# Block-product mixing in an adaLN block: sums and low parts moved to VectorE in pieces of 1536 columns

## The chip, the cores and the metric

The kernel runs on one core of a Trainium2 chip. The metric is the device time of one execution in microseconds (us), shown as the median of several runs. The engines are named as in the profile: PE (TensorE, matmuls), PEld (its weight loads), DVE (VectorE), ACT (ScalarE), POOL (GpSimd) and SP (SyncE, which here issues almost all DMAs). Each engine works through its own queue in order.

## What is computed

One transformer block on 2048 tokens of width 448, in float32: layernorm with modulation, attention with 16 heads of width 28, and a gated MLP whose gate mixes tokens with a 2048 x 2048 matrix.

```python
h = _layernorm(x) * (1 + ca) + sa
x = x + ga * _A_ref(h, A_wqkv, A_wo)             # attention, 16 heads
h = _layernorm(x) * (1 + cb) + sb
z = _gelu(h @ w_in)                              # 2048 x 1792
z1, z2 = z[:, :896], _layernorm(z[:, 896:])
g = w_sp @ z2 + b_sp[:, None]                    # the mixing, 2048 x 2048 by 2048 x 896
x = x + gb * ((z1 * g) @ w_out)
```

## The kernel before

The order on every engine is written out by hand, and the pools of buffers set the waits. A product of two float32 operands is made of three one-pass matmuls in `F32R`: each operand is split into a high part (`hi`, a rounded copy made by ACT) and a low part (`lo`, the operand minus `hi`, made by DVE or POOL in `sub`), and PE sums hi by hi, hi by lo and lo by hi.

The stages follow each other on PE: projections and the first row maxima; attention (256 slots of 4 score tiles, 4 tiles for the row maxima of a later head, and 4 products with V; a slot is one head and one block of 128 keys); the output projection; z1 (28 units of 11 matmuls, `z1_unit`, from weights `w_in`); z2 (16 tiles, `z2_gemm` and `z2_norm`); the mixing; and y, the product with `w_out` (16 tiles of 21 matmuls, `y_part`).

The mixing does not multiply 4 x 4 blocks of `w_sp` (512 x 512 each) with the blocks of z2 directly. For two of three column groups of z2 (384 columns each) it uses 26 products of sums of blocks, listed in `MIX`: each entry holds the sums of z2 blocks to form (`T0`, `T1` are kept, `ONCE` is used by one product only), the block that is multiplied and its sign, the weight (an index into `W_SUMS` for a sum of blocks of `w_sp`, or a pair for a plain block), and the output blocks (column group c, token block tb, sign) to which the product is added. A product p is four steps g = 4p + kt (kt the block of 128 rows), and a step is 9 matmuls of 512 columns into three PSUM banks. The third group of 128 columns (`F6_AT`) adds 3 matmuls to 64 of the 104 steps. So the stage has 104 x 9 + 64 x 3 = 1128 matmuls. Products with even and odd p use two sets of three banks. Per step the loop calls, in this order: `w_load(g + 4)` (SP), `w_split(g + 2)` (hi and lo of the weights), `z_split(g + 4)` (hi and lo of one 384-column piece of z), `evac(p - 1, kt)` (adds one bank of the product before to its outputs `cE`, `cC`, `cF`, `cD`), `z_sum(g + 6)`, gates, and the matmuls in `mix_step(g)`.

POOL makes the z sums (`z_sum`) and the low parts of the weights (`w_split`); DVE makes the low parts of z (`z_split`) and of the third group's weights, and all additions to the outputs. For weights that are sums, the low parts of kt 0 and 1 come ready from DRAM (`wl_scr`), so only kt 2 and 3 have a low part to make. Weight tiles go through few buffers:

```python
PARTS = {"h": (2048, 5), "l": (4608, 4), "p": (6144, 3)}   # hi, lo, ready lo: offset, buffers
raws[g] = [wp.tile([128, 512], F32, name="raw_sp", bufs=5)]
```

The sums of `w_sp` blocks are made during attention: `ws_load` (two loads), `ws_add` (POOL, for 44 of the 112 pieces also hi and lo), `ws_store`, with three pairs of buffers. Attention also needs POOL for the row maxima of each head: `m_max` (DVE, then three short POOL instructions, `mxv` and `mxp`) and in the same slot `m_fin` (a PE transpose `mtp`, a DVE copy `nt`, two small DMAs `qst<-nt` on SP that the head's scores wait for). The slot is the 13th of a head (12 modulo 16).

The output weights are split during the mixing and y starts (`wout_load`, `wout_gate`, `wout_part`); the gate by z1 (`gate`) and the split of the result (`u_split`, which makes `uT`) run tile by tile at the end of the mixing and between the y tiles.

Of the kernel before, what the change touches and what calls it, by code (L numbers as in the profile page):

```python
# [62 lines left out]

T0, T1, ONCE = 8, 9, 10
# [28 lines left out]
ROWS = (0, 2, 3, 1)  # L93
# [4 lines left out]
def tile_adaln_mha_gmlp(ctx, tc, x, wqkv, wo, w_in, w_spT, b_sp, w_out, cT, w_mod0, w_mod, out):  # L98
# [13 lines left out]
    ws_scr = scr.tile([4 * len(W_SUMS), 128, 512], F32, name="ws_scr")  # L112
    wl_scr = scr.tile([2 * len(W_SUMS), 128, 512], F32, name="wl_scr")
# [734 lines left out]
    ws_raw = spool.tile([128, 6, 512], F32, name="ws_raw")  # L848

    def ws_tiles(i):  # L850
        return [ws_raw[:, 2 * (i % 3) + j, :] for j in range(2)]

    def ws_load(i):
        v, kt = divmod(i, 4)
        for t, src in zip(ws_tiles(i), W_SUMS[v][:2]):
            sp.dma_start(t, ws_scr[4 * src + kt] if isinstance(src, int) else w_block(*src, kt))

    def ws_add(i):
        v, kt = divmod(i, 4)
        a, b = ws_tiles(i)  # L860
        pool.tensor_tensor(out=a, in0=a, in1=b, op=ALU.add if W_SUMS[v][2] > 0 else ALU.subtract)  # L861
        if v in W_OPERANDS and kt < 2:
            hi = b.bitcast(F32R)
            pool.tensor_copy(hi, a)
            sub(pool, hi, a, hi)

    def ws_store(i):
        v, kt = divmod(i, 4)
        a, b = ws_tiles(i)
        sp.dma_start(ws_scr[i], a)  # L870
        if v in W_OPERANDS and kt < 2:
            sp.dma_start(wl_scr[2 * v + kt], b)
# [290 lines left out]
    win_load(1, t3b)  # L1163
    for g in range(NG):
        for f in range(7):
            z1_unit(g, f)
            if g == 0 and f == 4:
# [53 lines left out]

    zt = [dpool.tile([128, 8 * 896], F32, name=f"z2{i}", tag=f"heapD{i}") for i in range(2)]
    z2 = [zt[i // 8][:, i % 8 * FH : (i % 8 + 1) * FH] for i in range(NT)]

    once = {}

    def z_reg(r, g):
        kt = g % 4
        if r == ONCE:
            return once[g]  # L1230
        if r >= T0:
            return tsum(r - T0)[:, kt * 384 : (kt + 1) * 384]
        return z2[4 * ROWS[r % 4] + kt][:, FG[r // 4]]

    def z_sum(g):
        if g >= KS:
            return
        for d, a, b, op in MIX[g // 4][0]:
            if d == ONCE:
                once[g] = wp.tile([128, 384], F32, name="once")  # L1240
# [4 lines left out]
    def z_split(g):  # L1245
        if g >= KS:
            return
        _, r, sign, _, _ = MIX[g // 4]
        src, (hi, lo) = z_reg(r, g), zs(g)
        if sign > 0:  # L1250
            act.activation(hi, src, AF.Copy)
            sub(dve, lo, src, hi)
        else:
            act.activation(hi, src, AF.Copy, scale=-1.0)
            dve.scalar_tensor_tensor(out=lo, in0=src, scalar=-1.0, in1=hi.bitcast(F32), op0=ALU.mult, op1=ALU.subtract)
        once.pop(g, None)

    def z6_split(t):
        act.activation(z6h[:, t, :], z2[t][:, FG[2]], AF.Copy)
        sub(dve, z6l(t), z2[t][:, FG[2]], z6h[:, t, :])  # L1260
# [34 lines left out]
    def w_split(g):  # L1295
        for key, eng in ((g, pool), (("f", g), dve)):
            if key in raws:
                raw = raws.pop(key)
                hi = w_part("h")
                act.activation(hi, raw[0], AF.Copy)  # L1300
# [32 lines left out]

    for t in range(NT + 1):
        if t < NT:
            z2_gemm(t)
        if 0 < t <= NT:
            z2_norm(t - 1)
        if t == 8:
            heapB2.append(fh.tile([128, 8 * 896], F32R, name="heapB2", tag="heapB"))  # L1340
            tbuf.append(wp.tile([128, 5120], F32, name="tbuf", tag="tw", bufs=1))
        if 9 <= t < 13:
            z_sum(t - 9)
            b_load(bts(t - 9), t - 9)
        if 10 <= t < 14:
            z_split(t - 10)
        if t >= 9:
            z6_split(2 * t - 18)
            z6_split(2 * t - 17)
# [5 lines left out]
    for g in range(4, 6):  # L1355
        z_sum(g)
# [12 lines left out]
    acc, acc6 = {}, {}  # L1369
    F6_ENDS = {tb: (min(gs), max(gs)) for tb in range(4) for gs in [[g for g in F6_AT if F6_AT[g][0] == tb]]}  # L1370

    def mix_step(g):
        p, kt = divmod(g, 4)
        if p < 2 and kt == 0:
            acc[p] = [bank("acc") for _ in range(3)]
        zh, zl = zs(g)
        hi, lo = wsp.pop(g)
        for f in range(3):
            c, o = slice(f * 128, (f + 1) * 128), acc[p % 2][f]
            pe.matmul(o, zh[:, c], hi, start=p < 2 and kt == 0, stop=False, skip_group_check=p > 1)  # L1380
            pe.matmul(o, zh[:, c], lo, start=False, stop=False, skip_group_check=p > 1)  # L1381
            pe.matmul(o, zl[:, c], hi, start=False, stop=kt == 3, skip_group_check=p > 1)  # L1382
        if g in F6_AT:
# [3 lines left out]
            side = tb in (2, 3)  # L1387
            if side not in acc6:
                acc6[side] = ps_o.tile([128, 512], F32, name="acc6", tag="o") if side else bank("acc6")
            o, t = acc6[side], 4 * ROWS[k] + kt  # L1390
# [8 lines left out]
    def evac(p, f):  # L1399
        for c, tb, sign in MIX[p][4]:  # L1400
            u = utile(3 * c + f, tb)
            d_add(u, u if (c, tb) in started else bts(tb), acc[p % 2][f], ALU.add if sign > 0 else ALU.subtract)
            if f == 2:
                started.add((c, tb))
# [21 lines left out]
    def u_split(f, tb):  # L1426
        if tb not in uTs:
            uTs[tb] = hview(dpool.tile([128, 8 * 896], F32R, name="uT", tag=f"heapD{(1, 0, 1, 0)[len(uTs)]}"), 0, 14, 512)
        uT, u = uTs[tb], utile(f, tb)
        act.activation(uT[:, f, :], u, AF.Copy)  # L1430
        sub(dve, uT[:, 7 + f, :], u, uT[:, f, :])

    x2t, yps = {}, {}

    wraws = {}

    def wout_load(f):
        wraws[f % 2] = wp.tile([128, D], F32, name="wraw_o", bufs=2)
        sp.dma_start(wraws[f % 2], w_out[f * 128 : (f + 1) * 128, :])

    def wout_gate(f):
        d_add(wraws[f % 2], wraws[f % 2], bcs["gb"], ALU.mult)

    def wout_part(f):
        if f == 0:
            tbuf.append(wp.tile([128, 5120], F32R, name="wouts", tag="tw", bufs=1))
        act.activation(wouts_h(f), wraws[f % 2], AF.Copy)
        sub(dve, wouts_l(f), wraws[f % 2], wouts_h(f))
# [5 lines left out]
    def y_part(t, end=False):  # L1454
        ts, uT = slice(t % 4 * 128, t % 4 * 128 + 128), uTs[t // 4]
        y = bank("y_ps")
# [9 lines left out]
    GATE_AT = (69, 70, 71, 76, 77, 79, 81, 83, 92, 93, 94, 95, 96, 97, 98, 99, 100)  # L1466
    WOUT_LOAD = (48, 49, 60, 61, 97, 99, 101)
    WOUT_GATE = (50, 51, 62, 63, 98, 100, 102)
    WOUT_PART = (51, 52, 63, 64, 100, 101, 103)

    for g in range(KS):
# [3 lines left out]
        z_split(g + 4)  # L1475
        if p and kt < 3:
            evac(p - 1, kt)
        z_sum(g + 6)
# [6 lines left out]
        if g >= 97:  # L1485
            u_split((6, 3, 4, 5, 0, 1, 2)[g - 97], 2)
        for fn, at_g in ((wout_load, WOUT_LOAD), (wout_gate, WOUT_GATE), (wout_part, WOUT_PART)):
            if g in at_g:
                fn(at_g.index(g))
# [5 lines left out]
    ts = [8, 9, 10, 11, 4, 5, 6, 7, 12, 13, 14, 15, 0, 1, 2, 3]  # L1495
    splits = [(f, 1) for f in (6, 0, 1, 2, 3, 4, 5)] + [(f, 3) for f in (3, 4, 5, 0, 1, 2, 6)] + [(f, 0) for f in (0, 1, 2, 6, 3, 4, 5)]
    for f in range(3):
        evac(NM - 1, f)
    for k, t in enumerate(ts):
        if k + 2 < len(ts):  # L1500
            x2_load(ts[k + 2])
        if k < 12:
            for _ in range((1, 1, 1, 1, 2, 2, 2, 1, 0, 0, 0, 0)[k]):
                gate()
                z1_load()
            for _ in range((2, 2, 2, 1)[k % 4]):
                u_split(*splits.pop(0))
        y_part(t, k == 15)

# [51 lines left out]
```

## Time and profile before

| | |
|---|---|
| time, three runs | 1414.46, 1417.89 and 1422.31 us; median 1417.89 |
| profiled execution | 1415.37 us, span 1413.6 us, mean granted clock 0.995 |
| busy | PE 1382.3, PEld 976.0, DVE 1086.3, ACT 816.7, POOL 535.8 us |
| moved by DMA | 247.89 MB |
| mixing on PE | from 1058.1 us of the span to 1341 us |

The profile has one row per group of instructions (line, engine, operation, output and input tiles, count, busy time, mean duration, idle time before and what ended it), a list of waits (who waited for whom: total, times, longest), and windows (busy time of each engine in a stretch, then the granted PE clock, the DMA share and GB/s). A PE that is 98% busy is the bound over most of the span; its matmuls overlap, so their mean duration (0.39 us for 512 columns) is longer than the distance from one to the next.

### The profile page before, as it was taken

How to read it: one execution, taken by the hardware profiler on the slowest of the kernel's cores; microseconds unless marked ns; L12 is line 12 of the kernel's file. 1: busy time of each engine (PE TensorE's matmuls, PEld its weight loads, DVE VectorE, ACT ScalarE, POOL GpSimd, SP SyncE). 2: the span in 40 equal slices, each digit the busy share in tenths (PEclk: the TensorE clock that was granted, in tenths of full speed). 3: DMA queues.
4: the chain of work that ended last, by engine and by line, in shares of the span. 5: the costliest groups of instructions: out<-in, count | busy, mean ns of one | idle time of the engine just before them, and what ended most of it. 6: DMA issues, size and time to landing. Idle time of an engine off the chain costs nothing. (4 is left out here: it accounts for less than half of the span.)

```text
span 1413.6 us, 20902 instructions
## 1 busy us (share of the span) xinstructions
PE 1382.3 (98%) x7098; PEld 976.0 (69%) x7098; DVE 1086.3 (77%) x1788; ACT 816.7 (58%) x1578; POOL 535.8 (38%) x499
## 2 busy tenths in 40 slices
PE   9999999999999999999999999999999999888998
PEld 8888655555555555555555545888997888666798
DVE  7898888888888888888888841840469779987962
ACT  6623666777766666776776678452245545544421
POOL 2134334233436254344533351000149456844400
PEclk9999999999999999999999999999999999999999
DMA  7464756666666666666577542533206756676553
GB/s 276 142 182 171 211 143 179 184 174 199 187 193 174 199 195 188 189 175 192 185 201 215 187 155 73 177 130 124 89 16 218 220 181 208 200 229 192 182 182 98
DMA packets 133048, 247.89 MB, mean 175 GB/s; under 512 B 21385, under 2 KB 33291, under 8 KB 130395
## 3 DMA queue, kind: packets, MB, share of 16 engines
q1 hardware_dynamic: 130222, 242.37, 56.5%
q10 hardware_dynamic: 2718, 4.19, 0.8%
q8 instruction: 56, 0.92, 0.3%
q14 instruction: 52, 0.42, 0.1%
HBM read 171.32 MB, written 70.38 MB: 171 GB/s over the span
## 5 line engine op out<-in xcount | busy, mean ns | idle before, releaser
L710 DVE TENSOR_REDUCE pm<-mt 128x1 f32<-128x512 f32 x1024 | 631.3, 682 | 86.0 <-PE mt L705 86.0
L741 ACT ACTIVATE P<-st_ps 128x512 f32<-128x512 f32 x1024 | 515.7, 626 | 210.1 <-PE st_ps L737 209.4
L737 PE MATMUL st_ps<-qst,kst 128*128 128x512 f32 x1024 | 406.4, 406 | 3.3 <-DMA qst<-nt 2.8
L705 PE MATMUL mt<-kst,qst 128*128 128x512 f32 x1024 | 402.5, 393 | 0.0
L737 PEld LDWEIGHTS st_ps<-qst,kst 128*128 128x128 f32 x1024 | 191.2, 188 | 146.0 <-issue 96.2
L861 POOL TENSOR_TENSOR ws_raw<-ws_raw 128x512 f32<-128x512 f32 x112 | 144.2, 1288 | 323.6 <-DMA ws_raw<-in_w_spT_dram 177.4
L752 PE MATMUL o_ps<-P,V 128*32 128x512 f32 x2048 | 247.5, 601 | 0.0
L705 PEld LDWEIGHTS mt<-kst,qst 128*128 128x128 f32 x1024 | 192.4, 188 | 31.6
L1300 ACT ACTIVATE heapB<-raw_sp 128x512 fp32r<-128x512 f32 x156 | 97.5, 629 | 129.3 <-issue 41.9
L752 PEld LDWEIGHTS o_ps<-P,V 128*32 128x32 f32 x2048 | 53.7, 109 | 124.0 <-issue 118.6
L1380 PE MATMUL acc<-heapB,heapA 128*128 128x512 f32 x312 | 123.1, 395 | 11.3 <-ACT heapB L1300 5.6
L147 POOL TENSOR_TENSOR heapB<-raw_sp,heapB 128x512 fp32r<-128x512 f32 x60 | 85.2, 1424 | 109.4 <-ACT heapB L1300 91.1
L1382 PE MATMUL acc<-heapB,heapA 128*128 128x512 f32 x312 | 122.4, 392 | 0.0
L1381 PE MATMUL acc<-heapB,heapA 128*128 128x512 f32 x222 | 87.4, 394 | 8.4 <-DVE heapB L147 5.2
L1380 PEld LDWEIGHTS acc<-heapB,heapA 128*128 128x128 f32 x312 | 59.1, 190 | 27.4 <-ACT heapB L1300 7.7
L147 DVE TENSOR_TENSOR heapB<-raw_sp,heapB 128x512 fp32r<-128x512 f32 x52 | 53.8, 1034 | 22.4 <-ACT heapB L1300 21.2
L1382 PEld LDWEIGHTS acc<-heapB,heapA 128*128 128x128 f32 x312 | 59.0, 189 | 12.1
L400 PE MATMUL pq<-heapD,heapD 128*128 128x512 f32 x196 | 61.9, 390 | 0.0
L147 POOL TENSOR_TENSOR ws_raw<-ws_raw 128x512 fp32r<-128x512 f32 x44 | 56.5, 1285 | 3.5
L1320 DVE BATCH_NORM_STATS2 stz<-z 128x6 f32<-128x448 f32 x32 | 20.0, 626 | 47.8 <-ACT z L1319 47.5
L167 POOL TENSOR_TENSOR rsz<-rsz,mhalf 128x1 f32<-128x1 f32 x16 | 14.6, 914 | 109.0 <-DMA tbuf<-in_b_sp_dram 64.7
L1381 PEld LDWEIGHTS acc<-heapB,heapA 128*128 128x128 f32 x222 | 41.8, 188 | 18.9 <-DVE heapB L147 6.1
(224 smaller groups left out, 1832.0 us busy)
## 6 DMA issues: line engine op xcount, KB each, us to landing
ws_raw<-in_w_spT_dram SPq DMA_DIRECT2D x136, 256.0 KB
ws_scr<-ws_raw SPq DMA_DIRECT2D x112, 256.0 KB
ws_raw<-ws_scr SPq DMA_DIRECT2D x88, 256.0 KB
raw_sp<-ws_scr SPq DMA_DIRECT2D x88, 256.0 KB
raw_sp<-in_w_spT_dram SPq DMA_DIRECT2D x68, 256.0 KB
wl_scr<-ws_raw SPq DMA_DIRECT2D x44, 256.0 KB
kst<-qk_scr SPq DMA_DIRECT2D x45, 224.0 KB
qst<-qk_scr SPq DMA_DIRECT2D x45, 224.0 KB
```

Source lines behind the costliest of these rows:

```text
L147: eng.tensor_tensor(out=dst, in0=a, in1=hi.bitcast(F32), op=ALU.subtract)
L400: pe.matmul(pq, wqk[:, b, m * 128 : (m + 1) * 128], hT[g][:, a, :], start=j == 0, stop=j == NST - 1)
L705: pe.matmul(mt, qst[h % 3][:, t * 128 : (t + 1) * 128], kst[h % 3][:, kb * 512 : (kb + 1) * 512], start=True, stop=True)
L710: dve.tensor_reduce(out=pms[h][:, t, kb : kb + 1], in_=mt, axis=AX.X, op=ALU.max)
L737: pe.matmul(st, kst[h % 3][:, kt * 128 : (kt + 1) * 128], qst[h % 3][:, qb * 512 : (qb + 1) * 512], start=True, stop=True)
L741: act.activation(p, st, AF.Exp, scale=SCALE)
L752: pe.matmul(otile[h][32 * qb : 32 * qb + 32, :], V[:, kt, h, :], ptiles.pop((u, qb)), start=kt == 0, stop=kt == NT - 1)
L861: pool.tensor_tensor(out=a, in0=a, in1=b, op=ALU.add if W_SUMS[v][2] > 0 else ALU.subtract)
L1300: act.activation(hi, raw[0], AF.Copy)
L1380: pe.matmul(o, zh[:, c], hi, start=p < 2 and kt == 0, stop=False, skip_group_check=p > 1)
L1381: pe.matmul(o, zh[:, c], lo, start=False, stop=False, skip_group_check=p > 1)
L1382: pe.matmul(o, zl[:, c], hi, start=False, stop=kt == 3, skip_group_check=p > 1)
```

## The change

The matmuls and their order on PE stay the same. Around them:

- In the mixing POOL has nothing left to do: `z_sum`, `w_split` and all low parts go to DVE. Sums (`z_sum`), hi (`z_hi`, ACT) and lo (`z_lo`, DVE) of z are made for a whole product at once, four pieces of 384 = 1536 columns, and `evac` adds three banks at once: the accumulators become two tiles of three neighbouring banks (`accs`).
- The output weights are multiplied by `gb` and split in the z1 stage, stored in DRAM (`wo2_scr`) and loaded ready at steps 80 and 100 of the mixing (`wouts_load`).
- `u_split` works on up to three tiles at once, and y uses a ring of eight banks.
- In attention the sums of `w_sp` use six pairs of buffers, another order (`W_ORDER`) and other slots, nine of 16 from slot 2 on: the add 4 slots and the store 7 slots after the load (3 and 5 before).

```diff
-    ws_raw = spool.tile([128, 6, 512], F32, name="ws_raw")
+    ws_raw = []
     def ws_tiles(i):
-        return [ws_raw[:, 2 * (i % 3) + j, :] for j in range(2)]
+        if not ws_raw:
+            ws_raw.append(dpool.tile([128, 7, 512], F32, name="ws_raw", tag="heapF"))
+            ws_raw.append(spool.tile([128, 6, 512], F32, name="ws_raw2"))
+        k = i % 6 if i < 100 else 3 + i % 3
+        return [ws_raw[k // 3][:, 2 * (k % 3) + j, :] for j in range(2)]
...
-    for i, slot in enumerate([j for j in range(2, 256, 2) if j % 32 != 28][: 4 * len(W_SUMS)]):
+    for i, slot in enumerate([j for j in range(2, 256) if j % 16 in (0, 2, 3, 5, 6, 10, 11, 14, 15)][: 4 * len(W_SUMS)]):
         at(slot, ws_load, i)
-        at(slot + 3, ws_add, i)
-        at(slot + 5, ws_store, i)
+        at(slot + 4, ws_add, i)
+        at(slot + 7, ws_store, i)
...
-        at(200 + 8 * i, win_first, i)
+        at(212 + 8 * i, win_first, i)
...
+    def wout_load(f):
+        wouts[f] = [wo3.tile([128, D], F32, name="raw_out")]
+        sp.dma_start(wouts[f][0], w_out[f * 128 : (f + 1) * 128, :])
+    def wout_part(f):
+        raw = wouts[f][0]
+        dve.tensor_tensor(out=raw, in0=raw, in1=bcs["gb"], op=ALU.mult)
+        hi, lo = (wo3.tile([128, D], F32R, name=f"wout_{i}") for i in range(2))
+        act.activation(hi, raw, AF.Copy)
+        sub(dve, lo, raw, hi)
...
+    def wouts_load(i):
+        if i == 0:
+            tbuf.append(wp.tile([128, 5120], F32R, name="wouts", tag="tw", bufs=1))
+            sp.dma_start(hview(tbuf[1], 0, 7, D).bitcast(F32), wo2_scr[0].rearrange("f p n -> p f n"))
+            sp.dma_start(hview(tbuf[1], 3136, 4, D).bitcast(F32), wo2_scr[1, 0:4].rearrange("f p n -> p f n"))
...
-            pool.tensor_tensor(
-                out=z_reg(d, g), in0=z_reg(a, g), in1=z_reg(b, g), op=ALU.add if op > 0 else ALU.subtract
-            )
+            dve.tensor_tensor(out=z_reg(d), in0=z_reg(a), in1=z_reg(b), op=ALU.add if op > 0 else ALU.subtract)
...
+    def z_hi(p):
+        if p < NM:
+            act.activation(z_parts(p)[0], z_reg(MIX[p][1]), AF.Copy, scale=float(MIX[p][2]))
...
-        for key, eng in ((g, pool), (("f", g), dve)):
+        for key, eng in ((g, dve), (("f", g), dve)):
...
-    def evac(p, f):
+    def evac(p):
         for c, tb, sign in MIX[p][4]:
-            u = utile(3 * c + f, tb)
-            d_add(u, u if (c, tb) in started else bts(tb), acc[p % 2][f], ALU.add if sign > 0 else ALU.subtract)
+            u = (cE, cC, cF, cD)[tb][:, c * 1536 : c * 1536 + 1536].rearrange("p (f n) -> p f n", n=512)
+            first = bts(tb)[:, None, :].broadcast_to([128, 3, 512])
+            d_add(u, u if (c, tb) in started else first, accs[p % 2], ALU.add if sign > 0 else ALU.subtract)
...
         w_split(g + 2)
-        z_split(g + 4)
-        if p and kt < 3:
-            evac(p - 1, kt)
-        z_sum(g + 6)
+        if kt == 0:
+            if p:
+                z_hi(p + 1)
+                evac(p - 1)
+        elif kt == 1 and p:
+            z_lo(p + 1)
+        elif kt == 2:
+            z_sum(p + 2)
```

Two places show what stands in the queues. The first is DVE in product 13 of the mixing, before: `heapA` is a low part of z, `heapB` a low part of a weight, `cF` and `cD` are outputs that take product 12.

```order
L1367 TENSOR_TENSOR cF<-cF,acc 128x512
L1367 TENSOR_TENSOR cD<-cD,acc 128x512
L147 TENSOR_TENSOR wouts<-wraw_o,wouts 128x448
L147 TENSOR_TENSOR heapA_11189<-z_11190,heapA_11189 128x384
L1367 TENSOR_TENSOR cF<-cF,acc 128x512
L1367 TENSOR_TENSOR cD<-cD,acc 128x512
L147 TENSOR_TENSOR heapB_11509<-raw_sp,heapB_11509 128x512
L147 TENSOR_TENSOR heapA_11189<-z_11190,heapA_11189 128x384
L1367 TENSOR_TENSOR cF<-cF,acc 128x512
L1367 TENSOR_TENSOR cD<-cD,acc 128x512
L1367 TENSOR_TENSOR cF<-cF,acc_12499 128x512
```

The additions come bank by bank, and the sums and the other low parts of the weights stand on POOL. The same product on DVE after the change (the two `z` rows are the sums for product 15):

```order
L1413 TENSOR_TENSOR cF<-cF,acc_11860 128x1536
L1413 TENSOR_TENSOR cD<-cD,acc_11860 128x1536
L150 TENSOR_TENSOR heapB_11578<-raw_sp,heapB_11578 128x512
L150 TENSOR_TENSOR heapA_11258<-z_11259,heapA_11258 128x4x384
L150 TENSOR_TENSOR heapB_11578<-raw_sp,heapB_11578 128x512
L1279 TENSOR_TENSOR z_11260<-z_11260,z_11259 128x4x384
L1279 TENSOR_TENSOR z_11259<-z_11260 128x4x384
L1413 TENSOR_TENSOR cF<-cF,acc_11863 128x512
L150 TENSOR_TENSOR heapB_11578<-raw_sp,heapB_11578 128x512 x2
```

Everything stands in one queue now, in pieces three times as wide. The second place is POOL in attention before the change, up to the three `m_max` rows of a head (`ws_raw` is a sum of weights, `osb` the attention output of another head):

```order
L781 TENSOR_TENSOR osb<-osb,rb 128x512
L861 TENSOR_TENSOR ws_raw<-ws_raw 128x512 x2
L864 CAST ws_raw<-ws_raw 128x512
L147 TENSOR_TENSOR ws_raw<-ws_raw 128x512
L719 TENSOR_SCALAR mxv<-mxv 128x16
L720 CAST mxp<-mxv 128x16
L147 TENSOR_TENSOR mxp<-mxv,mxp 128x16
```

The add in front of them is placed one slot earlier than they are. After the change the last add in front of the same rows is placed two slots earlier:

```order
L784 TENSOR_TENSOR osb<-osb,rb 128x512
L868 TENSOR_TENSOR ws_raw_1696<-ws_raw_1696 128x512
L871 CAST ws_raw_1696<-ws_raw_1696 128x512
L150 TENSOR_TENSOR ws_raw_1696<-ws_raw_1696 128x512
L868 TENSOR_TENSOR ws_raw<-ws_raw 128x512
L722 TENSOR_SCALAR mxv<-mxv 128x16
L723 CAST mxp<-mxv 128x16
L150 TENSOR_TENSOR mxp<-mxv,mxp 128x16
```

The instructions are the same; their distance to the row maxima is what moved.

More of the change, by code (lines that the diff above doesn't have):

```diff
@@ L1386, in mix_step @@
                 hi, lo = wsp.pop(("f", g))
[L1387 to L1390, printed above, removed]
+            o, t = accs[3 if tb in (2, 3) else 2][:, 0, :], 4 * ROWS[k] + kt
             pe.matmul(o, z6h[:, t, :], hi, start=g == F6_ENDS[tb][0], stop=False)
@@ L1455, in y_part @@
         ts, uT = slice(t % 4 * 128, t % 4 * 128 + 128), uTs[t // 4]
-        y = bank("y_ps")
+        y = ring.tile([128, 512], F32, name="y_ps", tag=f"y{ts_order.index(t) % 8}")
         for f in range(7):
@@ L1484, in tile_adaln_mha_gmlp @@
             gate()
[L1485 to L1489, printed above, removed]
+        if g == 80:
+            wouts_load(0)
+        if g == 100:
+            wouts_load(1)
+        if g in SPLIT_AT:
+            u_split(2, SPLIT_AT[g])
         if g >= KS - 2:
```

152 lines of the change are left out of this document (80 added, 72 removed).

## The prediction

> **What bounds the kernel now.** I read the page's busy times first, then the windows of the mixing stage, then the waits of PE.
>
> ```profile
> PE 1382.3 (98%) x7098; PEld 976.0 (69%) x7098; DVE 1086.3 (77%) x1788; ACT 816.7 (58%) x1578; POOL 535.8 (38%) x499
> 1100.00:1120.00 20.00, 20.00 (x90) 16.58 (x89) 11.98 (x19) 11.11 (x22) 5.15 (x4) 1.00 0.73 224
> 1220.00:1240.00 20.00, 16.91 (x68) 13.35 (x67) 19.54 (x22) 9.25 (x18) 18.20 (x14) 0.91 0.54 168
> 1260.00:1280.00 20.00, 11.23 (x42) 8.10 (x43) 14.28 (x16) 5.43 (x11) 10.59 (x8) 0.97 0.55 171
> L1380 PE MATMUL acc<-heapB,heapA x312: 388/389/632, 1058.1 to 1340.1; 128*128 128x512 f32 x156
> L1382 PE MATMUL acc<-heapB,heapA x312: 387/389/632, 1058.6 to 1340.6; 128*128 128x512 f32 x156
> 1301.98 0.23 PE acc L1391
> 1308.33 0.23 PE acc L1381
> ```
>
> PE is busy in 1382 of 1413.6 us, its instructions do not change, and so 31 us of idle time and whatever it loses to a lowered clock is all there is to win. A window's columns are its length and the busy time of PE, PEld, DVE, ACT and POOL, then the granted clock, DMA share and GB/s. In a good stretch of the mixing PE runs 90 matmuls in 20 us; in two bad ones 68 and 42, with the clock at 0.91 and 0.97. How much the stage loses follows from the other rows: between the two rows of the chain lie 28 distances in 6.35 us, 0.2268 us each. The stage has 1128 matmuls, so a dense one would go from its first start to its last in 1127 x 0.2268 = 255.6 us. The starts stand at 1058.1 and 1340.6, 282.5 us. The mixing therefore loses **26.9 us**. What ends PE's waits there, and in attention:
>
> ```profile
> PE acc L1380 <- ACT heapB L1300: 5.6, 5, 1.3
> PE acc L1381 <- DVE heapB L147: 5.2, 2, 3.5
> PE acc L1381 <- POOL heapB L147: 3.1, 3, 1.9
> PE acc L1380 <- DVE cF L1367: 3.1, 1, 3.1
> PE acc L1380 <- DVE cD L1367: 2.7, 2, 1.4
> PE st_ps L737 <- DMA qst<-nt: 2.8, 2, 2.4
> PE mtp L726 <- POOL mxp L147: 1.9, 3, 0.8
> PE st_ps L737 <- DVE pm L710: 0.6, 1, 0.6
> ```
>
> The first five, all of the mixing, are 19.7 us and end with a part of a weight (`heapB`) or with an addition that frees a bank (`cF`, `cD`); the rest of the 26.9 is shorter pauses and slow matmuls after pauses (0.632 us at most, against 0.389). The last three belong to attention, 5.3 us. Why are the parts late although DVE is not full in every bad window?
>
> ```profile
> L147 DVE TENSOR_TENSOR heapB<-raw_sp,heapB 128x512 fp32r<-128x512 f32 x52 | 53.8, 1034 | 22.4 <-ACT heapB L1300 21.2 <-issue 1.0
> L147 POOL TENSOR_TENSOR heapB<-raw_sp,heapB 128x512 fp32r<-128x512 f32 x60 | 85.2, 1424 | 109.4 <-ACT heapB L1300 91.1 <-issue 10.7 <-DMA raw_sp<-ws_scr 4.5
> L147 DVE TENSOR_TENSOR uT<-cE,uT 128x512 fp32r<-128x512 f32 x7 | 4.6, 690 | 4.4 <-ACT uT L1430 4.4
> L1367 DVE TENSOR_TENSOR cC<-cC,acc 128x512 f32<-128x512 f32 x28 | 18.7, 676 | 3.8 <-PE acc L1393 3.8
> 1309.94 0.68 DVE L147 TENSOR_TENSOR heapB<-raw_sp,heapB 128x512 fp32r<-128x512 f32 x1
> 1311.41 1.37 DVE L147 TENSOR_TENSOR heapB<-raw_sp,heapB 128x512 fp32r<-128x512 f32 x1 [0.32 <-ACT heapB L1300]
> ```
>
> The same subtraction on DVE takes 0.68 us or 1.37 us. It takes 0.69 us throughout at the end of the kernel, where POOL stands still, and an addition that reads an accumulator takes 0.676 us although POOL runs. So DVE work with both inputs outside the accumulators waits for a POOL instruction to end, and POOL's own takes 1.42 us. The weights' low parts thus cost double on one engine or the other.
>
> **The change, part by part.**
>
> *Mixing on DVE alone.* POOL has no instruction there any more, so I price DVE work at the undisturbed rows:
>
> ```profile
> L147 DVE TENSOR_TENSOR heapF<-raw,heapD 128x384 fp32r<-128x384 f32 x2 | 1.0, 552 | 0.0
> L147 DVE TENSOR_TENSOR heapF<-raw_in,heapD 128x896 fp32r<-128x896 f32 x2 | 2.2, 1092 | 13.3 <-ACT heapD L154 13.3
> 1337.70 0.61 DVE L1367 TENSOR_TENSOR wraw_o<-wraw_o,bc_gb 128x448 f32<-128x448 f32 x1
> 1338.24 0.61 DVE L147 TENSOR_TENSOR heapA<-wraw_o,wouts 128x448 fp32r<-128x448 f32 x1
> ```
>
> From 384 to 896 columns the time grows by 0.54 us, 1.055 ns a column; instructions in a row start 0.07 us before the one ahead has ended (0.54 us apart at 0.61 us). So 512 columns cost 0.62 less a little, I take 0.60, and 1536 columns 0.552 + 1152 x 0.001055 - 0.07 = 1.70; I take 1.68. `MIX`, `F6_AT` and the loop give the counts within the stage: 35 additions, 16 sums and 24 low parts of z of 1536 columns, 75 x 1.68 = 126 us; 60 low parts of weights, 52 of the third group's weights and 25 others (gates, splits, the third group's additions) of 512 columns, 137 x 0.60 = 82 us. DVE then works **208 us in a stage in which PE needs 256**.
>
> A mean does not show a queue, so I add up each product: PE needs 36 matmuls plus 3 for each step with the third group, 8.2 to 10.9 us. DVE needs more than PE in four of 26 products: 1 (10.8 against 9.5), 13 (12.0 against 9.5), 16 (11.4 against 9.5) and 19 (11.0 against 9.5), together 7.2 us. DVE can start at most about two steps ahead, since four low-part buffers serve up to two parts a step. I followed products 13 to 15, from the end of product 12 as zero: two additions end at 4.6, a weight part at 5.2, the low part of z at 6.9, two sums at 10.9, the third group's addition at 11.5, the next two additions at 16.1, and the weight part for the last step of product 14 at 16.7, where PE wants it at 17.0. The low part for product 15 ends at 19.0 and is wanted at 19.7. It holds, by 0.3 us. Bounds for what the stage still loses: 0 if the queue catches up every time, 7.2 us if nothing is caught up. I take 3.5, the middle, because a margin of 0.3 us leaves no room for the time between one engine's end and the next one's start. Gain 26.9 - 3.5 = **23.4 us**.
>
> *ACT.* A split of 512 columns and one of 896:
>
> ```profile
> L1300 ACT ACTIVATE heapB<-raw_sp 128x512 fp32r<-128x512 f32 x156 | 97.5, 629 | 129.3 <-issue 41.9 <-PE acc L1382 25.4 <-PE acc L1393 21.0
> L154 ACT ACTIVATE heapD<-raw_in 128x896 fp32r<-128x896 f32 x3 | 2.8, 945 | 0.0
> ```
>
> At 0.82 ns a column 1536 cost 1.47 us, where four of 384 cost about 2. `z_hi` waits for the product before to end, and a weight's hi for the next step but one waits behind it, 2.1 us after the product's start; DVE is in its additions then. Nothing on the path.
>
> *z1 and z2.* The split of the output weights (7 times two DVE and one ACT instruction, about 0.6 us each, 7 loads and 14 stores on SP) goes into z1, and the first sums and parts of z into z2:
>
> ```profile
> 900.00:1000.00 100.00, 100.00 (x486) 85.58 (x485) 41.14 (x88) 44.68 (x70) 5.41 (x6) 1.00 0.39 138
> L1320 DVE BATCH_NORM_STATS2 stz<-z 128x6 f32<-128x448 f32 x32 | 20.0, 626 | 47.8 <-ACT z L1319 47.5
> L1329 DVE TENSOR_SCALAR z<-z,mvz,rsz 128x896 f32<-128x896 f32 x16 | 11.8, 739 | 0.0
> ```
>
> In that window DVE and ACT work less than half the time and the DMAs have a share of 0.39, so 13 us spread over 70 are covered. An SP store that waits for DVE holds up a z1 store by at most a unit, and four z1 buffers stand between that and PE. A z2 tile costs DVE about 2.4 us against 22 matmuls of 0.2 on PE, 4.5 us; two sums (3.4 us) delay one tile's norm by 1.3 us, and no matmul waits for it. Cost 0; without the cover the two sums would be 3.4 us once.
>
> *The end.* A tile of y is 21 matmuls and ends with a DVE addition that waits for it:
>
> ```profile
> 1343.00:1411.00 68.00, 66.92 (x329) 61.70 (x329) 32.38 (x53) 12.09 (x21) 0.00 (x0) 1.00 0.44 142
> 1401.44 0.62 DVE L1463 TENSOR_TENSOR x2l<-x2l,y_ps 128x448 f32<-128x448 f32 x1 [3.63 <-PE y_ps L1460]
> 1405.70 0.62 DVE L1463 TENSOR_TENSOR x2l<-x2l,y_ps 128x448 f32<-128x448 f32 x1 [3.63 <-PE y_ps L1460]
> ```
>
> The tiles are 4.26 us apart, 0.203 us a matmul, and DVE is half idle. Its wide splits cost at most 1.68 + 2 gates + 1 addition = 3.5 us in a tile of 4.2, and each group is ready four tiles early. From the last matmul of the mixing (1341 us) to the last of y, 336 x 0.203 = 68.2 would do where 68.8 stand: gain **0.6 us**.
>
> *Attention.* The 5.3 us of waits are for POOL's row maxima behind a weight sum and for the small `nt` copies behind SP's weight traffic. The add is now two slots ahead (5.7 us, against 1.3 to 3.2 us of POOL work), a store no longer waits on a fresh add, and the sums are done by slot 205, before the last head's maxima. Against it: the same DMAs in 203 slots instead of 241. Bounds: 5.3 us gained, or as much lost if the denser traffic delays the copies as often; nearer to the gain, as PE waited for nothing else there: **4 us**.
>
> *Sum.* 1415.4 - 23.4 - 0.6 - 4 = 1387.4 for a run like the profiled one, which lies 2.5 us below the median of the three. Their spread of 8 us should shrink with the stalls, so I add little: **1388 us**. With every stall gone it would be 1415.4 - 26.9 - 0.6 - 5.3 = 1382.6.
>
> **The rivals.**
>
> *A burst of output weights.* `wouts_load(0)` puts 7 + 4 tiles of 224 KB, 2.5 MB, on SP's queue at step 80; before, the weights came in single tiles of that size.
>
> ```profile
> GB/s 298 268 258 258 277 256 166 200 206 223 90 171 235 161 159 116 194 109 184 277 245 179 179 289 107 207 208 202 109 209 152 170 138 264 368 292 348 22 0 112
> ```
>
> Those are the 40 slices from 1240 to 1341 us. At the best, 368, the burst takes 6.9 us, at their mean of about 200 12.6. Weight tiles asked for behind it are wanted some 7 us later at the earliest. If they stand behind all of it, PE loses 0 to 6 us once. The Trainium skill (DMA: Bandwidth & Descriptors, section Queues, rings and completion order) says that descriptors of one queue are consumed in ring order on each DMA engine; by that rule they do stand behind it. No run here has such a burst. Price +5 us: 1393. Chance 0.22.
>
> *The stalls move rather than go.* DVE, ACT and PE still hand each other few buffers, and in the window at 1260 no engine was full. If that loop and not POOL sets the pace, half of the 26.9 us stays: about 1400. For it: the waits for `ACT heapB`. Against it: windows like that at 1100, dense with the same buffers while POOL is nearly idle (5 of 20 us). Chance 0.10. If all of it stays, and DMA in attention gives nothing, no change: 0.07.
>
> *VectorE becomes the bound.* If something other than POOL doubles DVE's time, 40 sums and parts of 1536 and 137 of 512 columns at 1.37/0.69, the queue is 134 + 59 + 164 = 357 us and the kernel 75 us slower, 1490. It decides against the change from 283 us of DVE work on, 36% over my price. Against it: 0.61 and 0.69 us in the last stage, with ACT and PE running. Chance 0.06.
>
> **Chances and range.** My forecast, 1381 to 1392, has 0.55, the burst 0.22, half the stalls 0.10, no change 0.07, slower 0.06. The range of 80% leaves out the last two and little else: 1380 to 1406. A change under 0.5% (7 us) could not be told from none: faster 0.87, same 0.07, slower 0.06.
>
> **What the changed profile would show.** Right: no POOL rows in the mixing but the z2 norms' powers; DVE's 512-column parts at 0.69 us and its 1536-column rows near 1.75; DVE about 80% busy between the stage's ends, and these 256 to 262 us apart; no `mtp <- POOL` waits. Wrong: 1536-column rows above 2.3 us; PE waits of several us near step 84 (with PE's clock below 1) that end with a DMA; a granted clock of 0.9 in the mixing's windows.

## The result and the profile after

The changed kernel takes 1407.05 us (median of six runs, 1404.09 to 1408.56), the kernel before 1416.68 beside it: a ratio of 0.9925, with a 95% interval of 0.9905 to 0.9945. It is faster by 10 us, where the forecast of 1388 lies 29 below, and it stands 1 us above the predicted range. The profiled execution took 1407.85 us with a span of 1405.9. First the busy times, the stage's first and last starts and the windows (columns as in the prediction):

```profile
PE 1379.5 (98%) x7098; PEld 977.2 (70%) x7098; DVE 1069.5 (76%) x1688; ACT 805.4 (57%) x1472; POOL 360.3 (26%) x367
L1423 PE MATMUL acc<-heapB,heapA x312: 387/389/793, 1052.8 to 1331.0; 128*128 128x512 f32 x156
L1425 PE MATMUL acc<-heapB,heapA x312: 388/389/628, 1053.4 to 1331.5; 128*128 128x512 f32 x156
1060.00:1080.00 20.00, 20.00 (x90) 16.57 (x89) 17.25 (x17) 11.06 (x16) 0.00 (x0) 1.00 0.75 254
1180.00:1200.00 20.00, 20.00 (x90) 16.57 (x89) 19.97 (x19) 11.16 (x16) 0.00 (x0) 1.00 0.66 202
1220.00:1240.00 20.00, 20.00 (x90) 16.55 (x89) 16.76 (x19) 10.24 (x14) 0.00 (x0) 1.00 0.77 243
1240.00:1260.00 20.00, 13.37 (x44) 9.66 (x43) 13.41 (x18) 7.82 (x11) 0.00 (x0) 0.83 0.53 169
1260.00:1280.00 20.00, 13.57 (x52) 10.41 (x51) 11.39 (x12) 6.18 (x9) 0.00 (x0) 0.87 0.87 296
```

POOL is gone from the mixing, and PE is dense for the first 180 us, even where DVE has no gap (19.97 of 20 us). Then two windows with 44 and 52 of 90 matmuls stand where the kernel before had one with 42. From the first start to the last the stage still takes 278.7 us (1331.5 - 1052.8) against 282.5, where 255.6 would be dense: it loses 23.1 us, not the 3.5 of the prediction. What PE waited for there, and the rows of PE that follow a wait (start, duration, line, in brackets the wait and what ended it):

```profile
PE acc L1423 <- ACT heapB L1342: 8.9, 4, 5.2
PE acc L1424 <- DVE heapB L150: 6.7, 3, 3.6
PE y_ps L1486 <- DVE cE L1413: 1.8, 1, 1.8
...
1248.08 0.79 PE L1424 MATMUL acc<-heapB,heapA 128*128 128x512 f32 x1 [3.65 <-DVE heapB L150]
1254.21 0.64 PE L1424 MATMUL acc<-heapB,heapA 128*128 128x512 f32 x1 [1.75 <-DVE heapB L150]
1259.07 0.50 PE L1423 MATMUL acc<-heapB,heapA 128*128 128x512 f32 x1 [1.24 <-ACT heapB L1342]
1263.59 0.50 PE L1424 MATMUL acc<-heapB,heapA 128*128 128x512 f32 x1 [1.27 <-DVE heapB L150]
1276.31 0.79 PE L1423 MATMUL acc<-heapB,heapA 128*128 128x512 f32 x1 [5.16 <-ACT heapB L1342]
1290.58 0.50 PE L1423 MATMUL acc<-heapB,heapA 128*128 128x512 f32 x1 [1.24 <-ACT heapB L1342]
1302.32 0.50 PE L1423 MATMUL acc<-heapB,heapA 128*128 128x512 f32 x1 [1.24 <-ACT heapB L1342]
```

Seven waits, 15.5 us, all for a part of a weight, and no other wait between 1060 and 1330 us. They belong to steps 78, 79, 80, 81, 84, 88 and 92, and the code says why just these. `w_split(g + 2)` stands ahead of `mix_step(g)`, so the parts of three steps must lie in buffers at once. There are four buffers for low parts and five for high ones. A step with a matmul of the third group has two high parts, unless both matmuls use the same block; it has two low ones too, unless its own comes ready from DRAM. Steps 78 to 80 have 2 + 1 + 2 = 5 low parts for four buffers, steps 80 to 82 have six high parts for five, and so on: counting through all 104 steps gives these seven and no others. There the split for step g + 2 writes into a buffer that step g still has to read, so PE at step g waits for work meant for two steps later, and reads the later part. That is also a fault in the value: at these steps a product is formed with a part of another weight block. The work stands in the queues of DVE and ACT behind that of the step before, as at step 78 (`heapA` and the gate with `z1l` belong to step 77):

```profile
1244.46 1.75 DVE L150 TENSOR_TENSOR heapA<-z,heapA 128x1536 fp32r<-128x1536 f32 x1
1246.13 0.69 DVE L1413 TENSOR_TENSOR cF<-cF,z1l 128x512 f32<-128x512 f32 x1
1246.23 0.63 ACT L1342 ACTIVATE heapB<-raw_sp 128x512 fp32r<-128x512 f32 x1 [1.51 <-DVE heapA L150]
1246.73 1.29 DVE L150 TENSOR_TENSOR heapB<-raw_sp,heapB 128x512 fp32r<-128x512 f32 x2
```

The two `heapB` subtractions of the last row end at 1248.02, and PE goes on at 1248.08. The kernel before has the same buffers, the same order and the same steps. Its rows in the bad windows, which the prediction took for POOL and DVE holding each other:

```profile
1263.45 0.50 PE L1381 MATMUL acc<-heapB,heapA 128*128 128x512 f32 x1 [3.47 <-DVE heapB L147]
1268.23 0.50 PE L1381 MATMUL acc<-heapB,heapA 128*128 128x512 f32 x1 [1.76 <-DVE heapB L147]
1271.63 0.50 PE L1380 MATMUL acc<-heapB,heapA 128*128 128x512 f32 x1 [1.29 <-ACT heapB L1300]
1277.42 0.50 PE L1381 MATMUL acc<-heapB,heapA 128*128 128x512 f32 x1 [1.89 <-POOL heapB L147]
1287.87 0.50 PE L1380 MATMUL acc<-heapB,heapA 128*128 128x512 f32 x1 [1.29 <-ACT heapB L1300]
```

3.47, 1.76, 1.29 against 3.65, 1.75, 1.24: the same waits at the same steps, whoever makes the low part. At step 81 it is POOL before (1.89) and DVE after (1.27). How many matmuls they cost show its window at 1260 (42 of 90) and the next:

```profile
1280.00:1300.00 20.00, 17.42 (x71) 13.64 (x71) 13.34 (x20) 10.86 (x20) 5.70 (x5) 0.94 0.66 204
```

48 and 19 are missing, 67 x 0.2268 = 15.2 us; that leaves 11.7 of the 26.9 us for everything else.

The long wait at 1276 us has a second cause. SP issued the output weights (`wouts`) at 1260, and a raw tile asked for behind them came so late that ACT stood 5.26 us:

```profile
1260.22 0.43 SPq L1254 DMA_DIRECT2D wouts<-wo_scr  x1
1260.70 0.56 SPq L1255 DMA_DIRECT2D wouts<-wo_scr  x1
1272.32 0.63 ACT L1342 ACTIVATE heapB<-raw_sp 128x512 fp32r<-128x512 f32 x1 [5.26 <-DMA raw_sp<-ws_scr]
1274.98 1.27 ACT L1342 ACTIVATE heapB<-raw_sp 128x512 fp32r<-128x512 f32 x2 [0.69 <-DMA raw_sp<-ws_scr]
```

So the theory to test (A): what remains is the short rings, made longer by the load at step 80. The rivals: VectorE is late at these steps whatever the rings (B); the load alone causes the stretch (C); and, for the kernel before, the prediction's account of POOL and DVE.

### The profile page after: what moved, and what is told of

It is laid out like the page before. It is cut to its first block, busy times and chain, and to the rows that moved or that the text cites. A ratio compares the mean times of both kernels' runs of the same rounds, so it can differ in the third digit from the quotient of the medians.

```text
span 1405.9 us, 20520 instructions
## 1 busy us (share of the span) xinstructions
PE 1379.5 (98%) x7098; PEld 977.2 (70%) x7098; DVE 1069.5 (76%) x1688; ACT 805.4 (57%) x1472; POOL 360.3 (26%) x367
## 5 line engine op out<-in xcount | busy, mean ns | idle before, releaser
L150 DVE TENSOR_TENSOR heapB<-raw_sp,heapB 128x512 fp32r<-128x512 f32 x112 | 75.0, 688 | 47.1 <-ACT heapB L1342 46.4
L784 POOL TENSOR_TENSOR osb<-osb,rb 128x512 f32<-128x512 f32 x15 | 19.2, 1282 | 111.2 <-DMA rb<-r_scr 65.9
L1361 ACT ACTIVATE z<-z_ps 128x448 f32<-128x448 f32 x32 | 17.4, 545 | 46.8 <-PE z_ps L1358 46.8
```

The lines of the kernel that those rows point to most:

```text
L150: eng.tensor_tensor(out=dst, in0=a, in1=hi.bitcast(F32), op=ALU.subtract)
```

## The experiments

Each ratio is to runs of the kernel before on the same chip, whose medians were 1421.50 us beside the first four experiments of the table, 1418.19 beside the next four and 1420.63 beside the last three. "Mixing to y" goes from the first matmul of the mixing to the first of y in the profiled execution; dense it is 255.6 + 0.2 = 255.8 us.

| kernel | median us | ratio (95%) | mixing starts, us | mixing to y, us |
|---|---|---|---|---|
| before | 1416.68 | | 1058.09 | 282.7 |
| after | 1407.05 | 0.9925 (0.9905 to 0.9945) | 1052.83 | 280.9 |
| longer rings | 1393.68 | 0.9801 (0.9777 to 0.9825) | 1052.22 | 265.6 |
| spread load | 1404.92 | 0.9887 (0.9862 to 0.9911) | 1054.38 | 276.0 |
| both | 1387.87 | 0.9761 (0.9738 to 0.9784) | 1054.68 | 259.0 |
| before, late split | 1407.22 | 0.9904 (0.9881 to 0.9928) | 1061.98 | 273.8 |
| after, late split | 1398.20 | 0.9867 (0.9838 to 0.9896) | 1052.63 | 269.9 |
| both, weights' low parts on POOL | 1391.14 | 0.9808 (0.9782 to 0.9835) | 1052.44 | 263.7 |
| both, attention as before | 1393.57 | 0.9833 (0.9805 to 0.9861) | 1057.78 | 259.3 |
| both, y in the accumulators | 1398.37 | 0.9867 (0.9840 to 0.9894) | 1050.32 | 258.0 |
| both, y in three banks | 1385.47 | 0.9762 (0.9740 to 0.9785) | 1050.77 | 258.6 |
| both, sums and low parts on POOL | 1398.89 | 0.9853 (0.9829 to 0.9877) | 1050.99 | 271.4 |
| both, again (control) | 1387.04 | 0.9769 (0.9747 to 0.9791) | 1050.76 | 259.4 |

**Longer rings.**

```diff
-    PARTS = {"h": (2048, 5), "l": (4608, 4), "p": (6144, 3)}
+    PARTS = {"h": 6, "l": 5, "p": 3}             # the sixth and the fifth in a tile of their own, 4 KB a partition
+    extra = wp.tile([128, 1024], F32R, name="extra", bufs=1)
...
-        (3, [g for g in range(80, 96) if g % 4 != 3], 24),
+        (3, (80, 81, 84, 85, 86, 88, 89, 90, 92, 93, 94, 95), 24),
```

Steps 80 to 82 need six low parts, so one block of the third group moves from step 82 to step 95.

> The changed kernel with longer rings for the weight parts: six high and five low buffers instead of five and four, and the fourth-column block of step 82 done in step 95. In the changed kernel the parts for step g + 2 are written ahead of step g's products, and at seven steps (78, 79, 80, 81, 84, 88, 92) into a buffer that step g has still to read, so that TensorE waits there for work two steps ahead; in this kernel no step shares a buffer with a later one before it has been read (the products then also read their own parts at those steps). Theory A (short rings): the seven waits of TensorE between 1248 and 1303 us (3.65, 1.75, 1.24, 1.27, 5.16, 1.24, 1.24 us, 15.5 us together, and some 7 us at a lower granted clock behind them) vanish but for what the load of output weights at step 80 leaves at step 84; the time is 1386 to 1395 us. Theory B (VectorE cannot keep up at these steps, the rings do not matter): the waits move a step and stay, 1402 to 1408. Theory C (the load of 2.5 MB at step 80 delays the weight tiles, and this causes the stretch): the waits up to 1259 us vanish at most, the one of 5 us stays, 1395 to 1402.

Six of the seven waits are gone, and from the mixing to y it is 15.3 us shorter. One is left, now at step 85, behind the load:

```profile
PE acc L1427 <- ACT heapB L1346: 4.6, 1, 4.6
1240.00:1260.00 20.00, 20.00 (x90) 16.57 (x89) 17.37 (x20) 8.62 (x12) 0.00 (x0) 1.00 0.74 247
1260.00:1280.00 20.00, 15.38 (x56) 12.12 (x55) 13.45 (x14) 10.63 (x15) 0.00 (x0) 0.83 0.89 292
```

Theory A holds and B falls: with the same work on DVE the window from 1240 is dense.

**Spread load.**

```diff
-            sp.dma_start(hview(tbuf[1], 0, 7, D).bitcast(F32), wo2_scr[0].rearrange("f p n -> p f n"))
-            sp.dma_start(hview(tbuf[1], 3136, 4, D).bitcast(F32), wo2_scr[1, 0:4].rearrange("f p n -> p f n"))
+        if i < 11:
+            t = wouts_h(i) if i < 7 else wouts_l(i - 7)
+            sp.dma_start(t.bitcast(F32), wo2_scr[i // 7, i % 7])
...
-        if g == 80:
-            wouts_load(0)
-        if g == 100:
-            wouts_load(1)
+        if g >= 80 and g % 2 == 0:
+            wouts_load((g - 80) // 2)
```

> The changed kernel with the output weights loaded tile by tile, one of 0.23 MB at every second step from 80 on, instead of two transfers of 2.5 MB together at step 80. Theory A (short rings, the load only lengthens one of the seven waits): the wait of 5.16 us at step 84 falls to 1.2 to 1.8 us like its neighbours at 88 and 92, the other six stay; 1400 to 1404 us. Theory C (the load causes the stretch): 1388 to 1396. Theory B (VectorE is late, the load is hidden): no change, 1405 to 1409.

```profile
PE acc L1425 <- DVE heapB L150: 6.6, 3, 3.6
PE acc L1424 <- ACT heapB L1343: 5.4, 4, 1.7
```

The wait of 5.16 us is 1.70 now, and the other six are what they were. The load does not cause the stretch (C falls), it comes on top of it. The time is 1 us above the range of A, on a chip where the kernel before is 4.8 us slower as well; from the mixing to y it is 4.8 us shorter.

**Both.** The two edits together.

> The changed kernel with the longer rings and the output weights loaded tile by tile. Theory A: no wait of TensorE over 0.5 us between 1060 and 1330 us, the mixing some 256 to 259 us long instead of 278; 1385 to 1389 us. Theory B: 1402 to 1408. Theory C: the same as with the spread load alone.

```profile
PE acc L1429 <- DVE extra L150: 0.9, 1, 0.9
1240.00:1260.00 20.00, 20.00 (x90) 16.58 (x89) 18.38 (x22) 9.52 (x14) 0.00 (x0) 1.00 0.71 236
1260.00:1280.00 20.00, 19.11 (x85) 15.51 (x84) 17.03 (x17) 11.57 (x17) 0.00 (x0) 1.00 0.94 302
```

1387.87 us, and 259.0 us from the mixing to y, of which 1.85 are the wait for y's banks: the stage itself loses 1.3 us. No wait over 0.5 us was expected, and two are there: the one for y, and 0.9 us at step 87 for a low part of DVE. Beside it on the same chip, the load at step 80 costs 1393.68 - 1387.87 = 5.8 us with long rings.

**Late split**, in the kernel before and in the changed one.

```diff
-        w_split(g + 2)
+        if g not in LATE:                        # LATE = (78, 79, 80, 81, 84, 88, 92)
+            w_split(g + 2)
 ...
         mix_step(g)
+        if g in LATE:
+            w_split(g + 2)
```

> The kernel before, where at the seven steps 78, 79, 80, 81, 84, 88, 92 the parts of step g + 2 are made behind step g's products instead of ahead of them (so that these steps also read their own parts); GpSimd and VectorE share the splitting as before. Theory A (short rings): the missing 15 us between 1260 and 1300 us (67 of 180 products) mostly come back, the some 12 us at 1060 to 1080, 1200 to 1240 and 1300 to 1320 us stay; 1403 to 1410 us. The prediction's account (GpSimd and VectorE hold each other, 26.9 us in all): no change, 1414 to 1420.

```profile
1220.00:1240.00 20.00, 16.90 (x71) 13.54 (x70) 20.00 (x24) 10.08 (x19) 16.67 (x13) 0.94 0.55 179
1260.00:1280.00 20.00, 19.49 (x85) 15.50 (x84) 19.24 (x23) 9.74 (x18) 14.13 (x10) 1.00 0.60 198
1280.00:1300.00 20.00, 17.44 (x71) 12.54 (x70) 15.78 (x23) 10.80 (x21) 9.64 (x7) 1.00 0.76 230
```

The order of one call at seven of 104 steps is worth 14.3 us in the kernel before (1421.50 to 1407.22; 10 to 17 by the interval), with POOL and DVE sharing as ever. The profiled execution is the slowest of the six, 1413.81 us, and its stage 8.9 us shorter. The window at 1260 has 85 matmuls instead of 42, with POOL busier than before (14.13 us against 10.59); the next one still has 71, with waits of 1.08 us for POOL and 1.19 us for an addition. So in this execution 43 of the 67 missing matmuls are back, 9.8 us. The window at 1220 stays bad, where DVE has no gap at all.

> The changed kernel with its short rings as they are (five high, four low buffers), but at the seven steps 78, 79, 80, 81, 84, 88, 92 the parts of step g + 2 are made behind step g's products instead of ahead of them, the edit of the run on the kernel before. Theory A (what costs is the order of the code, by which the products wait for the split of two steps on): nearly as good as longer rings, which gave 1394; 1391 to 1399. Rival (the number of buffers itself costs, whatever the order: the split then waits for the products and the next products for the split): 1400 to 1408.

In the changed kernel the same edit gives 1398.20, within the range of theory A; a wait of 6.6 us behind the load stays. The order of the code is a large part of the cause: from the mixing to y it wins 11.0 of the 15.3 us that longer rings win, and by the ratios, on different chips, 8 of 18 us. The rest stays with the short rings in this order too, so the rival is right in part.

**Contention**: the low parts of the steps' own weights back on POOL, then the sums too.

```diff
-        for key, eng in ((g, dve), (("f", g), dve)):
+        for key, eng in ((g, pool), (("f", g), dve)):
...                                                  # the second run has this too
-            dve.tensor_tensor(out=z_reg(d), in0=z_reg(a), in1=z_reg(b), op=ALU.add if op > 0 else ALU.subtract)
+            pool.tensor_tensor(out=z_reg(d), in0=z_reg(a), in1=z_reg(b), op=ALU.add if op > 0 else ALU.subtract)
```

> The kernel with longer rings and spread output weights (1388), where the low parts of the steps' own weight blocks are made on GpSimd again, as in the kernel before; the sums and the low parts of z2 stay on VectorE at 1536 columns. Nothing but the hold between the two engines and GpSimd's own pace is then added. The prediction's account (each 512-column subtraction that meets the other engine takes 1.37 instead of 0.68 us and this alone cost the kernel before up to 26.9 us): 1405 to 1415. Theory A (that account covers only the some 12 us outside the stretch of the short rings): 1392 to 1400. No contention that reaches TensorE: 1387 to 1390.

> The kernel with longer rings and spread output weights, where GpSimd makes both the sums of z2 (now 1536 columns at once) and the low parts of the steps' own weight blocks, as it did in the kernel before. The prediction's account (GpSimd and VectorE hold each other, and this cost the kernel before 26.9 us in the mixing): 20 to 27 us above the control. Theory A (26.9 us were some 12 to 15 of this contention and the rest the short rings): 8 to 16 us above. No contention that reaches TensorE: 0 to 3 us above.

> The kernel with longer rings and spread output weights once more, unchanged, as the control for the runs beside it on the same chip: 0.976 of the kernel before (0.974 to 0.978), no wait of TensorE over 1 us in the mixing.

The control has a wait of 1.32 us at step 87, where none over 1 us was expected. DVE's rows for the same subtraction in the mixing come first with both edits, then with the low parts on POOL, then with the sums too; the last two rows are POOL's sums and low parts in that third run:

```profile
L150 DVE TENSOR_TENSOR heapB<-raw_sp,heapB 128x512 fp32r<-128x512 f32 x69 | 46.7, 686 | 20.8 <-ACT heapB L1347 20.7
```

```profile
L150 DVE TENSOR_TENSOR heapB<-raw_sp,heapB 128x512 fp32r<-128x512 f32 x35 | 30.0, 856 | 22.3 <-ACT heapB L1347 22.2
```

```profile
L150 DVE TENSOR_TENSOR heapB<-raw_sp,heapB 128x512 fp32r<-128x512 f32 x35 | 48.5, 1393 | 21.2 <-ACT heapB L1347 21.1
L1284 POOL TENSOR_TENSOR once<-z 128x1536 f32<-128x1536 f32 x4 | 14.4, 3607 | 6.3 <-DVE heapA L150 6.3
L150 POOL TENSOR_TENSOR heapB<-raw_sp,heapB 128x512 fp32r<-128x512 f32 x36 | 56.0, 1558 | 57.8 <-ACT heapB L1347 57.7
```

The hold is real: 0.686, 0.856 and 1.393 us for the same work. POOL's work, that is the hold and POOL's own pace together, costs 11.9 us of the time (1398.89 against the control's 1387.04 on the same chip) and 12.0 us from the mixing to y (271.4 against 259.4). With the low parts alone it is 4.3 us there, and the time 1 us below the range of A. That is less than half of what the prediction put on it. With the 14.3 us of the late split it makes 26.2 of the 26.9 us, but the sum is no proof: the two come from different kernels (POOL's sums are 1536 columns wide here and were 384), and the late split's profiled stage was only 8.9 us shorter.

**Attention as before**: three pairs of buffers, the old order and slots.

> The kernel with longer rings and spread output weights (1388), where the sums of weight blocks in the attention stage go through three pairs of buffers at every second slot in their old order, as in the kernel before. The prediction priced the six pairs at 4 us (of 5.3 us of waits): 1391 to 1393.5 by that. If the 5.3 us by which the changed kernel's mixing starts earlier came from elsewhere (the banks of the z2 stage, the moved splits of output weights): 1387 to 1389.

```profile
PE st_ps L740 <- DMA qst<-nt: 2.5, 2, 2.3
PE mtp L729 <- POOL mxp L150: 2.5, 3, 1.5
PE st_ps L740 <- DVE pm L713: 1.2, 1, 1.2
```

The 6.2 us of waits are back, where the changed kernel has 2.7 (one wait for `mxp`). The mixing starts at 1057.78, in the three kernels beside it on its chip at 1050.32 to 1052.63; the time is 6 us above the two runs of both edits, on other chips (9 to 10 us by the ratios). The buffers, order and slots together are worth 5 to 7.5 us by the starts, somewhat more than the 4 of the prediction. The starts are no sharper than that: the kernel with both edits begins its mixing at 1054.68 in one profiled execution and at 1050.76 in the other, on another chip.

**y's banks.** PE waits 1.85 us before its first y tile. The pool of y's banks opens when the accumulators' pool closes, and so behind DVE's last addition, though the first banks were read out a product earlier.

```diff
-        y = ring.tile([128, 512], F32, name="y_ps", tag=f"y{ts_order.index(t) % 8}")
+        b = ts_order.index(t) % 8
+        y = accs[b // 3][:, b % 3, :] if b < 6 else accs[b - 4][:, 0, :]
```

> The kernel with longer rings and spread output weights (1388), where the output products accumulate in the mixing's own accumulators instead of a new pool in the same banks. TensorE now waits 1.85 us at the start of that stage, since the new pool as a whole waits for VectorE's last sum of the mixing, though the first output tiles lie in banks that were read two products earlier; behind it the products run at a lower granted clock for some 3 us. If that wait goes: 1383.5 to 1386.5. If the first output tile then waits for something else that is as late (its low part, the output weights): 1387 to 1389.

A miss: the wait is gone, but eight others came. They stand at the second and third y tile of each three-bank tile, so a y tile now waits for the reading of its neighbour:

```profile
PE acc L1492 <- DVE x2l L1497: 9.9, 8, 3.1
```

With the first accumulator in a pool of its own, closed one addition earlier, and y in turns in its three banks:

> The kernel with longer rings and spread output weights, where the first accumulator of the mixing has a pool of its own, which closes before VectorE's last sum (product 25), and three output tiles take turns in its banks. If the 1.85 us wait at the start of the output stage is the new pool's wait for that last sum, it goes, and with it the some 3 us at half speed behind it: 2 to 4 us below the control. If three output tiles are too few (a tile is read 0.6 us after its products, which take 4.2 us): waits of TensorE for VectorE at the fourth and later tiles, and no gain or a loss, as with the shared tile, which cost 10 us of such waits.

Here the first wait is gone and only one of 0.6 us for a y tile is left. The time, 1385.47, is 1.6 us below the control, short of the 2 to 4 expected, and the intervals do not tell the two apart. It has the lowest median of this study, 2.4% below the kernel before and, by the ratios, some 1.6% below the changed one.

## Why the prediction was wrong

- **What fell: the cause of the 26.9 us.** The prediction asked why the parts are late although DVE is not full, saw the subtraction at 0.68 and 1.37 us, and put the whole loss on POOL and DVE. Its term of 23.4 us (26.9 - 3.5) measured 3.8. POOL's work costs 11.9 us, with the hold and its own pace. The stretch from 1260 to 1300 us, 15.2, was in the main the rings, of which undoing the order alone won 14.3 by the medians and 8.9 by the profiled stage. The seven steps wait in both kernels, so the change could not win them. The hint was in its own rows: the window at 1260 has the fewest matmuls, and there neither DVE (14.28) nor POOL (10.59 of 20 us) is full, while the one at 1220, with DVE at 19.54 and POOL at 18.20, loses much less. An engine that makes others wait by being slow is busy; a loop of waits leaves all of them idle.
- **The step where it could have been seen**: "DVE can start at most about two steps ahead, since four low-part buffers serve up to two parts a step". The two numbers were put side by side but not multiplied out: the split stands ahead of the products, so three steps need up to six. A wait for a buffer had no term in the sum, which allowed for DVE's queue alone (0 to 7.2 us).
- **The residual of 3.5 us** fits the total by luck. With rings and load out of the way the mixing to y takes 259.0 and 259.4 us where the prediction's sum is 255.8 + 3.5 = 259.3, but 1.85 of it is y's wait, which was not foreseen; 1.3 and 1.7 us are left, within the bounds of 0 and 7.2. Right were 512 columns at 0.688 us, 1536 columns at 1.75, DVE 77% busy in the stage (214.9 of 278.7 us), no POOL row, and products 1, 13 and 16 without a pause. Not right was that no `mtp` would wait for POOL: one does, 2.7 us. Of its own signs of being wrong two came: a wait of several us at step 84, and a clock of 0.83 and 0.87 in the two bad windows.
- **The burst** was a rival priced at 5 us and measured 5.8, on top and not instead. The wait that it lengthened ends with ACT, and ACT's wait with the raw tile. By the rule that the prediction cites from the Trainium skill (DMA: Bandwidth & Descriptors, section Queues, rings and completion order) the later tiles stand behind the burst; the 5.26 us of ACT agree. No run tells standing in order from sharing the DMA engines.
- **"The stalls move rather than go"** was the nearest rival, with the right place, and had a chance of 0.10. Its price, half of the 26.9 us, is near the 14.3 us that the late split won. It and the burst were priced as alternatives to each other, at 1400 and 1393; both came, and 1400 + 5.8 is near the 1407.05 measured. The dense window at 1100 was no argument against it: every step there has few enough parts.
- **Attention**, 4 us: 5.3 in the profiled start of the mixing, 5 to 7.5 by undoing it. **The end**, 0.6 us: from y's first start to the end of the span 72.8 us before, 72.2 after.
- **The sum**, from the two profiled executions: 5.3 us ahead of the mixing, 282.5 - 278.7 = 3.8 in it, 2.0 lost between its last matmul and y (0.2 us before, 2.2 after, by the wait for y's banks), 0.6 behind; 7.7 in all, as the spans say. Of the 3.8, POOL's work gives 11.9 and the load takes 5.8; the other 2.3 were not measured apart. Half the clock may be part of it: by the trace's clock record PE has it for 6.8 us of the stage before and 13.7 after.

## What to carry over

Where a split or load for step g + k stands in the code ahead of the use in step g, count the buffers for k + 1 whole steps at their fullest, not for the mean step. Where they do not suffice, step g reads what was written for a later step, and the wait looks like a slow engine, since the profile names the tile and the engine that ended it, and not the step that the work was for. Stalls that sit in a few fixed places while every engine has gaps are a loop of waits: look for what the places have in common in the code before pricing a faster engine. And a hold between two engines that doubles an instruction is worth only as much as reaches the bounding engine, here 11.9 us at most.

## What the runs showed of the hardware

A short wait can cost as much again through PE's clock, and the same wait does so in one run and not in another. The 1.85 us ahead of y, in both edits together and then in the changed kernel (windows of 4 us; the granted clock is the third number from the end):

```profile
1312.00:1316.00 4.00, 2.34 (x8) 2.12 (x9) 3.88 (x3) 0.00 (x0) 0.00 (x0) 0.81 0.47 178
1316.00:1320.00 4.00, 4.00 (x17) 3.63 (x17) 0.22 (x1) 0.00 (x0) 0.00 (x0) 0.77 0.20 66
```

```profile
1332.00:1336.00 4.00, 2.30 (x11) 2.15 (x12) 3.92 (x3) 0.00 (x0) 0.00 (x0) 1.00 0.11 42
1336.00:1340.00 4.00, 4.00 (x21) 3.70 (x21) 0.62 (x1) 0.67 (x1) 0.00 (x0) 1.00 0.25 87
```

The trace's clock record knows two values, 1.0 and 0.5, and has 0.5 for 3.41 us from 1314.47 in the first. So 4 x 0.19 + 4 x 0.23 = 1.68 us are lost. Nine of the profiled executions have this wait of 1.85 us. In five (longer rings, both, control, after with late split, weights' low parts on POOL) such a stretch of 3.41 us follows, and from y's first matmul to the end of the span it takes 73.4 to 75.0 us. In the other four none follows, and it takes 71.7 to 72.2. The Trainium skill (TensorE: Matmul & The Clock Gate, section Part 1: The HAM clock gate) has a free-running window of 3413 ns and half the clock after an idle one. The length of 3.41 us agrees with that figure. That a whole window must be idle does not fit: here a gap of 1.85 us, about half of one, sufficed in five of nine executions. The waits of 1.24 us at 1290 and 1302 us of the changed kernel left the clock at 1.00 in every window of 4 us from 1284 to 1308.
